# Half of x transposed by VectorE and by transfers inside SBUF, in a spectral mix with a dense layer

## The chip, the core and the metric

The kernel runs on one core of one Trainium2 chip. The metric is the device time of one execution in microseconds, the median of several runs. The engines are TensorE (PE, with its weight loads shown as PEld), VectorE (DVE), ScalarE (ACT), GpSimd (POOL) and SyncE (SP); DMA transfers are issued from queues of SP, ACT and POOL and carried by 16 DMA engines that they share. SBUF is the memory that the engines work in, with 128 partitions; PSUM, in eight banks, receives what PE computes.

## The reference

```
g = sigmoid((x * gate_w).sum(-1, keepdims=True))
a = irfft2(rfft2(x) * (w_r + 1j * w_i))          # over S = 2048 and D = 512
h = x @ w1 + b1                                  # D = 512 -> F = 1792
b = (h * tanh(softplus(h))) @ w2                 # Mish, F -> D = 512
out = g * a + (1 - g) * b
```

The kernel takes A_x for both branches. All inputs and the output are bfloat16.

## The kernel before

The 2048 rows of x lie in SBUF as 16 tiles of 128 rows (`xo`, 128 partitions x 16 x 512). Both branches need x transposed, with the 512 features on partitions: `xT` holds four blocks of 128 features (even and odd features of the two halves of D), each 2048 columns long. PE makes it (L466 to L482): for each pair of tiles, eight transposes of 128x128 (L476) into a PSUM bank, and an eviction on VectorE, or on ACT for some of the first (`evx`, L480).

**The dense branch** runs in four chunks of 512 rows (four tiles each). For a chunk, 14 groups of four matmuls (`mm1`, L773, contraction over the four feature blocks) give h in a bank; ACT adds the bias and applies Mish (L788) and writes `act`, which has three slots, so chunk c uses slot c % 3. Then for each tile, 14 matmuls (`mm2`, L803) with w2; the result is scaled by 1 - g (`bev`, L755) into `xo`.

**The spectral branch** splits the transform. Sums and differences of the two halves of `xT` (`ts`, `td`, L497) go to `Tb`, four tiles at a time. Then the row stage (`a1`, L512), whose two parts are added and subtracted on VectorE (`e1`, L525), the first column stage (`s1`, L538), an eviction to `Ybuf` (`e2`, L543) and writes to the scratch `scr1` in HBM (L547). When all are written, they are read back in another layout (L619) for the second column stage (`s2`, L635), the product with the filter on VectorE and POOL (L672 to L685), the inverse of it (`s2i`, L695), another trip through HBM (`scr2`, L705 and L710), and for each tile the last inverse stages (`s1i`, L723; `a1i`, L734), two scaled sums on VectorE (L745) and two additions on POOL (L751), which leave g * a in `ga`. A last addition (`sum`, L823) and a store (L760) end a tile; tiles 14 and 15 end with `fin` (L815).

**The gate** is one product with a running sum for each tile on VectorE (`gdot`, L553), a power on POOL (L559) and three small operations on VectorE; everything that scales by g or 1 - g waits for them.

**The order** is written down, not computed here. Every operation is a task with its engine, its dependences and the banks that it may use. The string `ORDER` (L258) lists all tasks in one sequence, two digits each, with the engine where there is a choice and the bank where one is taken; `schedule` (L216) reads it, and each engine runs its tasks in that sequence, waiting on semaphores for what a task needs. Each queue issues its transfers in the same way, so a transfer that has to wait holds up those behind it on its queue. SP issues nearly all loads, all scratch transfers and all stores; ACT's queue issues three of the w1 loads, POOL's one small load of the bias.

The loads on SP begin with tiles 0 to 1 and 2 to 3 of x, the constants `FMs`, a part of w1, tiles 4 to 7 and 8 to 11, two more parts of w1, and tiles 12 to 15. Then come the constants `GMs`, the gate's weights, 18 loads of the filter (`WT`, whole rows on every other one of 32 partitions), a part of `rt`, and w2 in two halves.

Of the kernel before, what the change touches and what calls it, by code (L numbers as in the profile page):

```python
# [13 lines left out]
NT = 16  # L14
# [151 lines left out]
class _Graph:  # L166
# [91 lines left out]
ORDER = (  # L258
    "0M0N0U047050P060O07080Q2z09000S0A010R0B0C0D0T020E0F030V0G0H0W0I0J0X0x60z50Y0yv0Z0K10v1146v212v1H30a1366l51I6q0"
    "14v0L7011Jv6m6n6w1Kv0b716o0c726p731L40d1M36r1N0e1W50f6s6t741Ov1V70g1560h1Pv1X6x0i6y6u16v7510j1Qa1Zv6z0k1701av1"  # L260
    "971Yv77318v761R41Av781B61Sv7920l0m0n7B01fv7A0o7D10p7C1gv0q1D70r1Cv7E1h30s1r42j1s61j7F20t21v0u1Ev7H00v22v1i17G1"
    "T7J31kv7I1U1lv2451F27K7L01mv1t1Gv2371uv7N47M1vv252Ov7O7b127v1wa2D37c2k28a26v7d07f22Nv7e2l1b67g1n42m2E11ca7h22F"
    "7j01d1ov1e7i1x62Hv7k1p342922Gv1ya1q7l52Av2Ia2Q41z2P17m2Z67n0202n2R2b2B2J22Tv7o2a72C2Sv7p12Ka2Uv2cv7r67q2dv2L2V"
    "27s2M2ev7t02Wv2f67u7v12o2X2ga2p7x52Y7w2h2q7z07y2i2r816802s8F1822t3578H48G362u398J28I373A8L58K2v3B8N63C388M0w8P"
    "18O2w8R28Q2x8T02y8S3D4308U3E63Mv8V38X13Nv8W8Y3Rv3Pg313F7P03G323Qv3Og7Q333H3Tg3Z33Sg7Ra3a13b8Z63iv3I57S08a3mv3J"
    "3jv7T3K3L3U3nv3kg3V47Ua7V33c3Xa3Wv3d3pg3Y3e03v43f3og3w644v7W3lg3x3y49v7Y13g7Xv3z3h3q45v7Z48v46g4028307aa4147g3"
    "r4843ta4Bg3sv4Ag3u4H485a4I24Qv86642434J4K4C4Uv4L874Rv89188a4Vv4Sg4D44Wg4M38b24Ea4N4Fa4Tg8c8A4G4Xg8d74O8Ba4P4Y8"
    "C08e4Z28f14av4ba8D8g4c8t18Ev8v28u8x08w4d8z18y4e9124f904g933929549497096992989B79A4h39C4p59D04qv4ia4x64r59E4yv4"
    "j75534s5D45L156a5Ev5T04z65Ma8h24u504t4k5Uv4wg5N14m5F34vg525V55O8i4l9fv5G5Q4ng515b78k04og8jv5W5P54g5I5Sg5H5768l"
    "5ca9ev5853g9g599F75Rg5A8mv5Kg9H49G5Y5Cg5d65X9J09I9hv5e9lv5j45r39K5Jg8n75sv5ka5Bg9kv5g5z35ag9m6745f5l568a5t19iv"  # L270
    "8o60v5m5hg9j5u5o5ig5v6908pa6F45n5Zg6135w8q26Ga5qg629nv6A645pg8r6B9ov635xg9p6C6N46V59qv6Oa9L78sv5yg6Wa66g6P69rv"
    "6X46Q6H26Eg6d09s6Y9M6S6I6Dg6R6ea6K65g6J9O19Nv6Ug6a6Mg6Z9P9uv9tv6cv9v6f56Tg9Qa9R46bv6g9xv6h6Lg9S6i9wv6kv9y9V06j"
    "g9T9U9Y29W9b79X9Z9a9c9d"
)
NBF = 14
GD_N = 8
E2P = 2.2
# [14 lines left out]
def _build(nc, A_x, A_w_r, A_w_i, B_x, B_w1, B_b1, B_w2, gate_w, out):  # L292
# [8 lines left out]
    with es:  # L301
        def sb(name, shape, dt):
            return es.enter_context(nc.sbuf_tensor(name, shape, dt))

        xo = sb("xo", [128, NT, 512], BF)
        xT = sb("xT", [128, 4, NT * 128], BF)
        Tg = sb("Tg", [128, 8192], BF)
# [40 lines left out]
        TT = Zb[:].rearrange("p a b c d e -> p (a b c d e)")[:, 0:2048].rearrange("p (s j n) -> p s j n", s=4, j=4)  # L348
        junk = Tg[:, 6144:6656]
# [38 lines left out]
        def mm(n):  # L388
            return n / 2400.0 + 0.0025
# [10 lines left out]
        def pe(name, dur, fn, **kw):  # L400
            return G.add(name, "pe", dur, fn, lat=0.17, **kw)
# [63 lines left out]

        for t0, h in ((0, 0), (0, 1), (2, 0), (2, 1), (4, None), (6, None), (8, None), (10, None), (12, None), (14, None)):  # L466
            pt = _Ps(SPEC[::-1])
            hs = (0, 1) if h is None else (h,)
            c0, nc_ = 2 * hs[0], 2 * len(hs)

            def f_tr(e, t0=t0, c0=c0, nc_=nc_, pt=pt):
                ins = None
                for i in range(2):
                    for c in range(c0, c0 + nc_):
                        o, d0 = ((c - c0) * 2 + i) * 128, 256 * (c // 2) + c % 2
                        ins = e.transpose(psb[:, pt.bank, o:o + 128], xo[:, t0 + i, d0:d0 + 255:2], ident[:, :])  # L476
# [14 lines left out]
        for t in range(NT):  # L491
            if t % 4 == 0:
                G.cur_prio = PR["sp"] + 0.9
                h = t // 4
                cols = slice(512 * h, 512 * h + 512)
                for (nm, o, op) in (("s", 0, ALU.add), ("d", 2, ALU.subtract)):
                    tt(f"t{nm}{h}", lambda o=o, hb=h % 2: Tb[:, hb, o:o + 2, :], lambda cols=cols: xT[:, 0:2, cols],  # L497
                       lambda cols=cols: xT[:, 2:4, cols], op, 1024, rate=2.0,
                       reads=[("xT", 4 * h + i, q) for i in range(4) for q in range(2)], writes=[("T", h % 2, nm)])
            if t % 2 == 0:  # L500
# [3 lines left out]
                for half in range(2):  # L504
                    pa = pas[half]

                    def f_a1(e, pa=pa, hb=hb, t=t, half=half):
                        ins = None
                        for i in range(2):
                            j0 = 128 * (t % 4 + i)  # L510
                            for r in range(2):
                                ins = e.matmul(ps[:, pa.bank, 256 * i:256 * i + 256].rearrange("p (s m) -> p s m", s=4)[:, r:4 - r:3 - 2 * r, :],  # L512
                                               Tb[:, hb, 2 * r + half, j0:j0 + 128], FMs[:, 2 * half + r, :], start=True, stop=True)
                        return ins

                    pe(f"a1{half}_{t}", 4 * mm(128), f_a1, reads=[("T", hb, "s"), ("T", hb, "d"), "FD"], writes=[("pa", t, half)], alloc=pa,
                       deps=e1s.get(t - 4, ()) if half == 0 else (), prio=PR["sp"] + 0.1 - 0.1 * half)
# [33 lines left out]
        for t in range(NT):  # L551
            G.cur_prio = PR["gate"] if t >= GD_N else 60.0
            G.add(f"gdot{t}", "dve", dve_dur(512),  # L553
                  lambda e, t=t: e.scalar_tensor_tensor(out=junk, in0=xo[:, t, :], scalar=1.0, in1=gwb,  # L554
                                                        op0=ALU.mult, op1=ALU.mult, accum_out=gdot[:, t:t + 1]),
                  reads=[("x", t), "gw"], writes=[("gd", t), "junk"], lock=True, deps=e1s[14] if t >= GD_N else ())

# [206 lines left out]
        for c in range(NCH):  # L764
            hb = c % 3
            G.cur_prio = PR["mm1"] - c
            for ft in range(NFT):
                pd = _Ps(DENSE[c])

                def f_mm1(e, c=c, ft=ft, pd=pd, cols=(0, 512), ks=range(4)):  # L770
                    ins = None
                    for i in ks:
                        ins = e.matmul(ps[:, pd.bank, cols[0]:cols[1]], w1_sb[:, i, 128 * ft:128 * (ft + 1)], xT[:, i, 512 * c + cols[0]:512 * c + cols[1]],  # L773
                                       start=(i == 0), stop=(i == 3))
                    return ins
# [8 lines left out]
                else:  # L784
                    pe(f"mm1_{c}_{ft}", 4 * mm(512), f_mm1, reads=[("xT", 4 * c + i, q) for i in range(4) for q in range(2)] + [("w1", ft, 0), ("w1", ft, 1)],
                       writes=[("pm", c, ft)], alloc=pd, deps=mm2s.get(c - 3, ()), prio=pr_m)
                G.add(f"mish_{c}_{ft}", "act", act_dur(512, True),
                      lambda e, ft=ft, pd=pd, hb=hb: e.activation(act[:, hb, ft, :], ps[:, pd.bank, :], AF.Mish, bias=b1f[:, ft:ft + 1]),  # L788
                      reads=[("pm", c, ft), "b1f"], writes=[("act", hb, ft)], frees=[pd], prio=PR["mish"])
            G.cur_prio = PR["mm2"] - c  # L790
            for tl in range(4):
                t = 4 * c + tl

                for part in range(len(LAST) if t == NT - 1 else 2):
# [5 lines left out]
                    def f_mm2(e, tl=tl, hb=hb, pd=pd, cs_=cs_, fts=fts):  # L800
# [8 lines left out]
                       writes=[("pd", t, part if t == NT - 1 else 0)],  # L809
                       alloc=pd if part == 0 or t == NT - 1 else None, deps=(mm2s[c][-1:] if t == NT - 1 and part else []))  # L810
                    mm2s.setdefault(c, []).append(tk)
# [126 lines left out]
```

## Time and profile before

| | us |
|---|---|
| median of 3 runs | 129.52 (129.48 to 129.56) |
| the profiled execution: span from its first to its last instruction | 128.0 |
| PE busy | 124.4 |
| VectorE busy | 92.2 |
| ACT busy | 68.9 |
| POOL busy | 54.4 |

The profile is one execution; its span leaves out what lies around the instructions, so it is shorter than the time of a run. A row of a group gives the line and the engine, what it writes and reads, the shape, how often, then the busy time in all and the mean of one in nanoseconds, and the idle time in front with what ended it. A piece of the chain of waits gives its start, its length and what it was, with the number of instructions merged into it. Spans of neighbouring instructions on an engine overlap: the mean of one is longer than the step from one start to the next. A row of a timeline has the start and the length first, and in brackets the idle time before. A row of a table by stages gives the stretch, its length, then the busy time of PE, PE's weight loads, VectorE, ACT and POOL with the number of instructions, the granted clock, the share of time in which the DMA engines are busy, and GB/s.

### The profile page before, as it was taken

The numbers are of one execution on the slowest core, as the hardware profiler recorded it, in microseconds if no ns is written. First come the engines' busy times: TensorE is split into PE (matmuls) and PEld (weight loads), VectorE is DVE, ScalarE is ACT, GpSimd is POOL, SyncE is SP. The second block draws the span as 40 slices with busy tenths as digits, with TensorE's granted clock in tenths as the row PEclk, the third lists the DMA queues.
The fourth block names the chain that finished last, engine by engine and source line by source line (L and its number), as shares of the span: only waits on it lengthen the run. The fifth ranks groups of instructions, "written<-read, shape, count | busy, mean of one in ns | idle before, by whom it ended". The sixth has DMA issues, their size and how long they took to land.

```text
span 128.0 us, 2725 instructions
## 1 busy us (share of the span) xinstructions
PE 124.4 (97%) x1046; PEld 67.9 (53%) x1046; DVE 92.2 (72%) x176; ACT 68.9 (54%) x113; POOL 54.4 (42%) x82
## 2 busy tenths in 40 slices
PE   7899999999999999999999999999999999999992
PEld 5698566545444444444444444444674457464482
DVE  0359997999989929998957900500399799999872
ACT  1339377889978784224024274487873475462300
POOL 4000000001000996979688394000038986998120
DMA  3999999999976398002304105449600204022231
GB/s 76 346 390 394 303 185 185 173 272 354 334 235 202 99 384 356 0 0 61 108 0 133 38 0 164 133 104 351 239 0 5 82 0 164 3 87 82 82 123 41
DMA packets 18653, 20.11 MB, mean 157 GB/s; under 512 B 1488, under 2 KB 15696, under 8 KB 18512
## 3 DMA queue, kind: packets, MB, share of 16 engines
q1 hardware_dynamic: 17792, 19.15, 49.7%
q10 hardware_dynamic: 816, 0.79, 1.9%
q8 instruction: 8, 0.13, 0.5%
q14 instruction: 5, 0.04, 0.1%
q0 software_dynamic: 32, 0.00, 0.0%
HBM read 13.64 MB, written 6.29 MB: 156 GB/s over the span
## 4 chain that ended last, share of the span: by engine, by line
PE 94%; DMA 3%; SPq 0%; DVE 0%; issue 0%
PE ps L803 38%; PE ps L773 38%; DMA xo<-in_A_x_dram 3%; PE ps L734 3%; PE ps L723 3%; PE ps L512 3%; PE ps L538 3%; PE ps L476 3%; PE ps L695 2%; PE ps L635 2%; SPq L374 0%; DVE xo L815 0%; PE ps L652 0%; PE ps L484 0%; PE ps L425 0%
## 5 line engine op out<-in xcount | busy, mean ns | idle before, releaser
L773 PE MATMUL ps<-xT,w_sb 128*128 128x512 bf16 (+1 forms) x240 | 52.9, 365 | 0.0
L803 PE MATMUL ps<-w_sb,act 128*128 128x512 bf16 (+2 forms) x252 | 51.6, 355 | 0.0
L788 ACT ACTIVATE act<-ps,b1f 128x512 bf16<-128x512 f32 x56 | 38.4, 688 | 18.5 <-PE ps L773 17.3
L803 PEld LDWEIGHTS ps<-w_sb,act 128*128 128x128 bf16 x252 | 22.7, 98 | 22.3 <-issue 0.8
L773 PEld LDWEIGHTS ps<-xT,w_sb 128*128 128x128 bf16 x240 | 22.3, 98 | 21.2 <-issue 0.6
L409 POOL TENSOR_TENSOR Tg<-Qb 128x256 bf16<-128x256 f32 x29 | 22.1, 790 | 21.9 <-DVE Qb L745 21.8
L409 POOL TENSOR_TENSOR Zb<-Qb 128x510 bf16<-128x510 f32 x16 | 19.8, 1268 | 5.1 <-DVE Qb L409 5.0
L409 DVE TENSOR_TENSOR Qb<-ps,WT 128x1024 f32<-128x1024 f32 x16 | 18.8, 1213 | 3.4 <-PE ps L635 3.4
L755 ACT ACTIVATE xo<-ps,omg 128x512 bf16<-128x512 f32 x8 | 5.5, 687 | 18.4 <-PE ps L803 10.1
L745 DVE SCALAR_TENSOR_TENSOR Qb<-ps,gcol,Qb 128x256 f32<-128x256 f32 x32 | 13.7, 475 | 1.5 <-ACT Qb L739 1.0
L404 DVE CAST Ybuf<-ps 128x1024 bf16<-128x1024 f32 x7 | 8.6, 1222 | 7.1 <-PE ps L695 6.7
L409 DVE TENSOR_TENSOR Abuf<-ps,Tg 128x512 bf16<-128x512 f32 x16 | 10.4, 685 | 2.4 <-PE ps L512 2.1
L576 POOL COPY wrv<-WT 128x32 bf16<-128x32 bf16 x2 | 0.4, 223 | 26.1 <-DMA WT<-in_A_w_i_dram 26.1
L405 ACT ACTIVATE Ybuf<-ps 128x1024 bf16<-128x1024 f32 x9 | 9.1, 1021 | 4.3 <-PE ps L695 4.3
L554 DVE SCALAR_TENSOR_TENSOR Tg<-xo,Tg 128x512 bf16<-128x512 bf16 x16 | 11.0, 688 | 0.3
L404 DVE CAST Zb<-ps 128x512 bf16<-128x512 f32 x6 | 4.1, 687 | 8.9 <-PE ps L723 8.9
L404 DVE COPY xT<-ps 128x1024 bf16<-128x1024 bf16 (+1 forms) x10 | 5.6, 579 | 5.4 <-PE ps L476 5.4
L409 DVE TENSOR_TENSOR xo<-xo,Tg 128x512 bf16<-128x512 bf16 x14 | 8.5, 615 | 0.3 <-ACT xo L755 0.3
L739 ACT ACTIVATE Qb<-ps,gcol 128x256 f32<-128x256 f32 x16 | 7.0, 475 | 2.7 <-PE ps L734 1.6
L405 ACT ACTIVATE Zb<-ps 128x512 bf16<-128x512 f32 x10 | 5.7, 596 | 4.6 <-PE ps L723 3.2
L598 POOL TENSOR_TENSOR ch<-wq 128x32 f32<-128x32 f32 x1 | 0.6, 624 | 12.5 <-DVE wq L593 12.5
L476 PE MATMUL ps<-ident,xo 128*128 128x128 bf16 x64 | 5.1, 225 | 0.5 <-DMA xo<-in_A_x_dram 0.5
(59 smaller groups left out, 92.8 us busy)
## 6 DMA issues: line engine op xcount, KB each, us to landing
Abuf<-scr SPq DMA_DIRECT2D x8, 512.0 KB, 5.4
scr<-Ybuf SPq DMA_DIRECT2D x16, 128.0 KB, 3.9
scr<-Ybuf SPq DMA_DIRECT2D x4, 512.0 KB, 3.8
w_sb<-in_B_w_dram SPq DMA_DIRECT2D x2, 896.0 KB, 13.6
out_dram<-xo SPq DMA_DIRECT2D x7, 256.0 KB, 2.0
xo<-in_A_x_dram SPq DMA_DIRECT2D x3, 512.0 KB, 7.7
rt<-c_rt SPq DMA_DIRECT2D x2, 512.0 KB, 8.5
WT<-in_A_w_r_dram SPq DMA_DIRECT2D x7, 128.5 KB, 10.4
```

The lines of the kernel that those rows point to most:

```text
L404: fs = {"dve": ("dve", dve_dur(n, rate=rate), lambda e: e.tensor_copy(out=dst(), in_=src())), "act": ("act", act_dur(n), lambda e: e.activ ...
L405: "act": ("act", act_dur(n), lambda e: e.activation(dst(), src(), AF.Copy))}
L409: f = lambda e: e.tensor_tensor(out=o(), in0=i0(), in1=i1(), op=op)
L476: ins = e.transpose(psb[:, pt.bank, o:o + 128], xo[:, t0 + i, d0:d0 + 255:2], ident[:, :])
L512: ins = e.matmul(ps[:, pa.bank, 256 * i:256 * i + 256].rearrange("p (s m) -> p s m", s=4)[:, r:4 - r:3 - 2 * r, :], Tb[:, hb, 2 * r + half ...
L554: lambda e, t=t: e.scalar_tensor_tensor(out=junk, in0=xo[:, t, :], scalar=1.0, in1=gwb, op0=ALU.mult, op1=ALU.mult, accum_out=gdot[:, t:t ...
L739: lambda e, t=t, sl=sl, p5=p5: e.activation(gC[:, sl, :].rearrange("p (i n) -> p i n", i=2), ps[:, p5.bank, :].rearrange("p (i n) -> p i n ...
L745: lambda e, t=t, sl=sl, p5=p5, o=o, op=op: e.scalar_tensor_tensor(out=st1[:, sl, o::2, :], in0=ps[:, p5.bank, :].rearrange("p (i n) -> p i ...
L755: G.add_multi(f"bev_{t}", [("act", act_dur(512, True), lambda e: e.activation(xo[:, t, :], ps[:, pd.bank, :], AF.Copy, scale=omg[:, t:t + ...
L773: ins = e.matmul(ps[:, pd.bank, cols[0]:cols[1]], w1_sb[:, i, 128 * ft:128 * (ft + 1)], xT[:, i, 512 * c + cols[0]:512 * c + cols[1]], sta ...
L788: lambda e, ft=ft, pd=pd, hb=hb: e.activation(act[:, hb, ft, :], ps[:, pd.bank, :], AF.Mish, bias=b1f[:, ft:ft + 1]),
L803: ins = e.matmul(ps[:, pd.bank, cs_], act[:, hb, ft, 128 * tl:128 * (tl + 1)], w2_sb[:, ft, cs_], start=(ft == 0), stop=(ft == NFT - 1))
```

## The change

Tiles 0 to 7 of x are still transposed by PE. Tiles 8 to 15 are transposed by VectorE in blocks of 32x32, one instruction for a tile, into a scratch that lies in slot 2 of `act` (the slot of chunk 2). Sixteen transfers of 64 KB inside SBUF then carry each group of 32 partitions of the scratch to the group of 32 partitions where it belongs in `xT`, eight issued on POOL's queue and eight on ACT's. Every one of them waits for all eight transposes.

`xT` is now two halves: `xTp` as before for tiles 0 to 7, and `xTb` for tiles 8 to 15, where the columns of a tile lie in four blocks of 32 by the group that they came from. What reads the second half follows: `mm1` of chunks 2 and 3 reads four runs of 128 columns and leaves its bank in that order, Mish reads the bank back in the order of rows, and the sums and differences `ts` and `td` of the second half are made in eight instructions of 512 columns (blocks of 32) instead of four of 1024. All of these wait for all sixteen transfers. The first eight Mish of chunk 2 wait for them too, since they write over the scratch.

Besides, the eight gate products that had to wait for the row stage need not any more, their scrap output has two buffers, and the pieces of tile 15's last `mm2` all come after the tile before. `ORDER` is new as a whole: the sequence on every engine, the banks, and the order of the loads. On SP the loads up to tiles 12 to 15 stay where they were; behind them the two halves of w2 and a part of `rt` come ahead of most of the filter loads, and the first writes to `scr1` stand between filter loads.

```
-        xT = sb("xT", [128, 4, NT * 128], BF)
+        xT = sb("xT", [128, 8192], BF)
...
+        xTp = xT[:, 0:4096].rearrange("p (q s) -> p q s", q=4)
+        xTb = xT[:, 4096:8192].rearrange("p (a q t j) -> p q a t j", a=4, q=4, t=8)
+        Zb32 = act[:, 2].rearrange("p f s -> p (f s)")[:, 0:4096]
+        Zw = Zb32.rearrange("p (b h e t j) -> p t h b e j", b=4, h=2, e=2, t=8)
...
-        for t0, h in ((0, 0), (0, 1), (2, 0), (2, 1), (4, None), (6, None), (8, None), (10, None), (12, None), (14, None)):
+        for t0, h in ((0, 0), (0, 1), (2, 0), (2, 1), (4, None), (6, None)):
...
+        for t in range(8, NT):
+            G.add(f"tp{t}", "dve", dve_dur(512), lambda e, t=t: e.transpose(
+                Zw[:, t - 8], xo[:, t, :].rearrange("p (b j e) -> p b e j", b=8, e=2)),
+                reads=[("x", t)], writes=[("Z", t)])
+        shs = []
+        for b in range(4):
+            for a in range(4):
+                shs.append(dma(f"sh{b}{a}", xT[32 * b:32 * b + 32, 4096 + 1024 * a:5120 + 1024 * a], Zb32[32 * a:32 * a + 32, 1024 * b:1024 * b + 1024],
+                               reads=[("Z", t) for t in range(8, NT)], writes=[("xB", b, a)], nbytes=65536, queue=SHQ[b], tail=1.9, bw=250e3))
+        XB = [("xB", b, a) for b in range(4) for a in range(4)]
...
+                    for e_ in range(2):
+                        xs = [xTb[:, e_ + 2 * i, :, 4 * h - 8:4 * h - 4, :] for i in range(2)]
+                        tt(f"t{nm}{h}{e_}", lambda o=o, e_=e_, hb=h % 2: Tb[:, hb, o + e_, :].rearrange("p (t a j) -> p a t j", t=4, a=4),
+                           lambda xs=xs: xs[0], lambda xs=xs: xs[1], op, 512, rate=2.0,
+                           reads=XB, writes=[("T", h % 2, nm, e_)])
...
-            G.cur_prio = PR["gate"] if t >= GD_N else 60.0
+            G.cur_prio = PR["gate"]
...
-                        ins = e.matmul(ps[:, pd.bank, cols[0]:cols[1]], w1_sb[:, i, 128 * ft:128 * (ft + 1)], xT[:, i, 512 * c + cols[0]:512 * c + cols[1]],
+                        o = ps[:, pd.bank, cols[0]:cols[1]]
+                        ins = e.matmul(o if c < 2 else o.rearrange("p (a t j) -> p a t j", a=4, t=4), w1_sb[:, i, 128 * ft:128 * (ft + 1)],
+                                       xTp[:, i, 512 * c + cols[0]:512 * c + cols[1]] if c < 2 else xTb[:, i, :, 4 * c - 8:4 * c - 4, :],
...
+                          act[:, hb, ft, :].rearrange("p (t a j) -> p t a j", t=4, a=4),
+                          ps[:, pd.bank, :].rearrange("p (t a j) -> p t a j" if c < 2 else "p (a t j) -> p t a j", t=4, a=4),
...
+                      deps=shs if c == 2 and ft < 8 else ())
```

with `SHQ = ("pool", "act", "pool", "act")`.

More of the change, by code (lines that the diff above doesn't have):

```diff
@@ L496, in _build @@
                 for (nm, o, op) in (("s", 0, ALU.add), ("d", 2, ALU.subtract)):
-                    tt(f"t{nm}{h}", lambda o=o, hb=h % 2: Tb[:, hb, o:o + 2, :], lambda cols=cols: xT[:, 0:2, cols],
-                       lambda cols=cols: xT[:, 2:4, cols], op, 1024, rate=2.0,
-                       reads=[("xT", 4 * h + i, q) for i in range(4) for q in range(2)], writes=[("T", h % 2, nm)])
+                    if h < 2:
+                        tt(f"t{nm}{h}", lambda o=o, h=h: Tb[:, h, o:o + 2, :], lambda cols=cols: xTp[:, 0:2, cols], lambda cols=cols: xTp[:, 2:4, cols], op, 1024, rate=2.0,
+                           reads=[("xT", 4 * h + i, q) for i in range(4) for q in range(2)], writes=[("T", h, nm, e) for e in range(2)])
+                        continue
+                    for e_ in range(2):
[3 more added lines that the diff above has]
+                           reads=XB, writes=[("T", h % 2, nm, e_)])
             if t % 2 == 0:
@@ L514, in f_a1 @@
                         return ins
-                    pe(f"a1{half}_{t}", 4 * mm(128), f_a1, reads=[("T", hb, "s"), ("T", hb, "d"), "FD"], writes=[("pa", t, half)], alloc=pa,
+                    pe(f"a1{half}_{t}", 4 * mm(128), f_a1, reads=[("T", hb, nm, half) for nm in "sd"] + ["FD"], writes=[("pa", t, half)], alloc=pa,
                        deps=e1s.get(t - 4, ()) if half == 0 else (), prio=PR["sp"] + 0.1 - 0.1 * half)
@@ L784, in _build @@
                 else:
[L785 removed]
+                    pe(f"mm1_{c}_{ft}", 4 * mm(512), f_mm1, reads=(XB if c >= 2 else [("xT", 4 * c + i, q) for i in range(4) for q in range(2)]) + [("w1", ft, 0), ("w1", ft, 1)],
                        writes=[("pm", c, ft)], alloc=pd, deps=mm2s.get(c - 3, ()), prio=pr_m)
                 G.add(f"mish_{c}_{ft}", "act", act_dur(512, True),
[L788 to L789 removed]
+                      lambda e, c=c, ft=ft, pd=pd, hb=hb: e.activation(
+                          act[:, hb, ft, :].rearrange("p (t a j) -> p t a j", t=4, a=4),
+                          ps[:, pd.bank, :].rearrange("p (t a j) -> p t a j" if c < 2 else "p (a t j) -> p t a j", t=4, a=4),
+                          AF.Mish, bias=b1f[:, ft:ft + 1]),
+                      reads=[("pm", c, ft), "b1f"], writes=[("act", hb, ft)], frees=[pd], prio=PR["mish"],
+                      deps=shs if c == 2 and ft < 8 else ())
             G.cur_prio = PR["mm2"] - c
@@ L809, in _build @@
                        writes=[("pd", t, part if t == NT - 1 else 0)],
[L810 removed]
+                       alloc=pd if part == 0 or t == NT - 1 else None, deps=(mm2s[c][-1:] if t == NT - 1 else []))
                     mm2s.setdefault(c, []).append(tk)
```

40 lines of the change are left out of this document (20 added, 20 removed).

## The prediction

> **What bounds the kernel now.** I read the page's totals first, then the granted clock, then the chain of waits.
>
> ```profile
> span 128.0 us, 2725 instructions
> PE 124.4 (97%) x1046; PEld 67.9 (53%) x1046; DVE 92.2 (72%) x176; ACT 68.9 (54%) x113; POOL 54.4 (42%) x82
> PE 94%; DMA 3%; SPq 0%; DVE 0%; issue 0%
> core 0: 128.0 us, clock 1.000
> ```
>
> A busy PE alone proves little, as matmul spans overlap. But the chain that ended last runs through PE for 94% of the span, at a full clock, so its start-to-start times are the price of each matmul:
>
> ```profile
> 5.57 0.40 PE ps L476 x4
> 7.12 1.75 PE ps L773 x16
> 10.42 0.45 PE ps L476 x8
> 36.51 0.43 PE ps L538 x2
> 36.94 4.32 PE ps L773 x20
> 47.36 0.56 PE ps L635 x32
> 90.83 0.45 PE ps L723 x8
> 119.56 6.13 PE ps L803 x56
> ```
>
> A 512-column matmul costs 4.32/20 = 0.216 us, a 256-column one 1.75/16 = 0.109, a transpose or other 128-column one 0.45/8 = 0.056. From 5.57 us the chain never leaves PE until 125.69 (119.56 + 6.13). So a matmul less is time less, as long as nothing makes PE wait. The only large hole is at the start, where PE waits for tiles 2 and 3 of x:
>
> ```profile
> 4.88 0.22 PE L425 MATMUL ps<-const-bfloat16-1.0 128*128 128x128 bf16 x1
> 5.57 0.40 PE L476 MATMUL ps<-ident,xo 128*128 128x128 bf16 x4 [0.48 <-DMA xo<-in_A_x_dram]
> ```
>
> **The change, part by part.** First, what leaves PE: eight tiles of four transposes, 32 x 0.056 = 1.79 us. Four of VectorE's ten evictions go with them. Second, the new order puts four 256-column matmuls (0.44 us) ahead of the transposes of tiles 2 and 3, inside that hole. They need the first half of w1, which came through ACT's queue:
>
> ```profile
> L374 ACTq DMA_DIRECT2D w_sb<-in_B_w_dram x3: 621/627/633, 0.8 to 2.1; - x3
> DMA to landing us min/median/max: 4.2/4.9/6.5
> ```
>
> The first was issued at 0.80 and landed at 0.80 + 4.2 = 5.0, so they run from 5.0 to 5.5 and the hole shrinks by about 0.44. PE's sum falls by 1.79 + 0.44 = 2.23.
>
> Third, what is added off PE. These are the rows nearest to each piece of work:
>
> ```profile
> L554 DVE SCALAR_TENSOR_TENSOR Tg<-xo,Tg 128x512 bf16<-128x512 bf16 x16 | 11.0, 688 | 0.3
> L404 DVE COPY xT<-ps 128x1024 bf16<-128x1024 bf16 x6 | 4.0, 683 | 0.0
> L409 DVE TENSOR_TENSOR Tg<-xT 128x1024 bf16<-128x1024 bf16 x8 | 5.3, 683 | 0.0
> L404 DVE COPY xT<-ps 128x512 bf16<-128x512 bf16 x4 | 1.6, 422 | 5.4 <-PE ps L476 5.4
> L404 DVE CAST Ybuf<-ps 128x1024 bf16<-128x1024 f32 x7 | 8.6, 1222 | 7.1 <-PE ps L695 6.7
> ```
>
> The trace has no transpose on VectorE. [...] I take 0.69, the gate's product, which like it handles 512 bf16 columns with no doubled rate. The eight cost 5.5 us; the evictions give back 4 x 0.683 = 2.7. The sums and differences of the second half become eight of 512 columns instead of four of 1024: 8 x 0.42 - 4 x 0.683 = +0.6 if their blocks of 32 columns keep the pace, +2.7 at 0.683 each. VectorE gains 3.4 us in all.
>
> Whether that costs time is a question of the feed. The sixteen transfers can start only when tile 15 is transposed. The loads ahead of the last x load on SP's queue are the same and in the same order, so I keep its landing:
>
> ```profile
> 5.47 0.78 SPq L374 DMA_DIRECT2D xo<-in_A_x_dram  x1
> DMA to landing us min/median/max: 9.5/9.5/9.5
> ```
>
> It lands at 5.47 + 9.5 = 15.0. VectorE's order puts the first four transposes before that and four behind it: 15.0 + 4 x 0.69 = 17.7. [...] Eight transfers then go out on POOL's queue, eight on ACT's with five Mish (128x512) among them:
>
> ```profile
> L374 POOL DMA_DIRECT2D braw<-in_B_b_dram x1: 785/785/785, 1.3 to 1.3; - x1
> braw<-in_B_b_dram POOLq DMA_DIRECT2D x1, 3.5 KB, 4.4
> L788 ACT ACTIVATE act<-ps,b1f 128x512 bf16<-128x512 f32 x56 | 38.4, 688 | 18.5 <-PE ps L773 17.3 <-PE ps L654 0.6 <-PE ps L585 0.2
> out_dram<-xo SPq DMA_DIRECT2D x1, 64.0 KB, 1.5
> ```
>
> POOL, at the one issue that the trace has: last issue at 17.7 + 7 x 0.785 = 23.2, landed 4.4 later, 27.6. That load had 14 rows, a transfer has 32, so the issue may cost up to 0.785 x 32/14 = 1.79; then 34.6. I take 0.8 to 1.0, nearer the row (29.1 at 1.0). ACT: last issue at 17.7 + 7 x 0.627 + 5 x 0.688 = 25.5. A landing takes between 1.5 (64 KB on idle engines) and 4.9 (256 KB on ACT's queue beside SP's loads); I take 2.5, since 64 KB is a quarter of that: 28.0, bounds 27.0 and 30.4.
>
> And the demand: in the new order PE has 78 matmuls of 512 columns, 28 of 256 and 52 of 128 between 5.57 and the first that reads tiles 8 to 15 (Matmult of chunk 2): 16.85 + 3.05 + 2.91 = 22.8 us, so it wants them at 28.4. Supply 28.0, demand 28.4: hidden, with half a microsecond to spare. If it is late, PE stalls at that matmul, its queue behind it holds the stage-one matmuls, and every microsecond passes to the end, because nothing later is slack. VectorE waits at the same point, with the stage-one evictions queued behind it. ACT's first issue waits on the transposes, with Mish of chunks 0 and 1 and so PE's banks behind it; it stands behind enough Mish to come up at about 17.7.
>
> [...]
>
> Fourth, what is moved. The column stage now ends later (laid out by the prices above, its last matmul ends at about 47, against 36.94), and PE has 44 matmuls of 512, 9.5 us, until it wants the data read back from scr, where before it had 10.4 (36.94 to 47.36). The chain there is an eviction of 1.0 to 1.2, two writes on SP and a read:
>
> ```profile
> L374 SPq DMA_DIRECT2D scr<-Ybuf x4: 615/616/617, 38.0 to 40.0; - x4
> DMA to landing us min/median/max: 2.1/2.2/2.6
> DMA to landing us min/median/max: 4.0/4.0/4.0
> ```
>
> (the last is the first read, Abuf<-scr at 42.3). 1.2 + 0.6 + 0.6 + 2.2 + 4.0 = 8.6: covered. The w2 loads move ahead of most filter loads on SP; the late filter loads have until about 49.7, when in the same layout the small filter matmul comes up. In the last stage PE's work from the first inverse matmul to the end falls from 34.9 (90.83 to 125.69) to about 28.3, while VectorE and POOL keep theirs:
>
> ```profile
> L409 POOL TENSOR_TENSOR Tg<-Qb 128x256 bf16<-128x256 f32 x29 | 22.1, 790 | 21.9 <-DVE Qb L745 21.8
> L745 DVE SCALAR_TENSOR_TENSOR Qb<-ps,gcol,Qb 128x256 f32<-128x256 f32 x32 | 13.7, 475 | 1.5 <-ACT Qb L739 1.0 <-PE ps L734 0.3 <-issue 0.2
> L409 DVE TENSOR_TENSOR xo<-xo,Tg 128x512 bf16<-128x512 bf16 x14 | 8.5, 615 | 0.3 <-ACT xo L755 0.3
> ```
>
> VectorE there: 13.7 + 8.5, five evictions (3.4), two adds (1.2), one scaling (0.75), the four last pieces (1.9): 29.5 busy, about 27 with the overlap of neighbours. It is as full as PE. So I take 0.6 of the 2.23 back for the tail and small waits (bounds 0 and 1.6). The profiled span was 128.0 and the median of the runs 129.52, 1.5 around it. Sum: 129.5 - 2.23 + 0.6 = **127.9**.
>
> **The rivals.** *Late feed* (the other side): POOL's software issue is the one price with wide bounds. At 1.79 us the last transfer lands at 34.6, PE stalls 6.2, and the time is 127.9 + 6.2 = 134; at 1.3 it lands at 31.2, stalls 2.8, 130.7. From 1.2 us an issue on (2 us of stall), the change loses. For it: 32 rows, DMA engines that are full in just this stretch, and at only 193 GB/s while narrow loads run (16 to 28 us):
>
> ```profile
> 1.00:16.00 15.00, 14.52 (x132) 10.84 (x131) 9.03 (x17) 6.74 (x12) 1.41 (x5) 1.00 0.97 322
> 16.00:28.00 12.00, 12.00 (x93) 6.93 (x92) 11.22 (x23) 9.45 (x17) 0.00 (x0) 1.00 1.10 193
> ```
>
> [...]
>
> *Slow sums*: blocks of 32 columns lose the double rate; 2.1 us more on VectorE between the transfers and the column stage, about half of it behind PE's other work: 127.9 + 1.0 = 128.9. Against it, nothing in the trace; for it, no row has such blocks.
>
> *The gain is eaten at the end*: VectorE, not PE, ends last. If its 27 us of the last stage start no earlier against PE and lose another 1.0 to 1.6 to POOL, the result is 128.9 to 129.6, say 129.3. For it: the sums on VectorE take 615 ns on average though one alone is shorter, while POOL runs beside them.
>
> **How the numbers follow.** Forecast 0.42, slow sums 0.10, late feed 0.33, tail 0.15. Some 0.2% (0.26 us) is what a measurement here can tell from no change. Faster: 0.42 + 0.10 + 0.05 of the tail + 0.02 of a slight late feed = 0.59. Same: 0.05 + 0.02 = 0.07. Slower: 0.29 + 0.05 = 0.34. The range runs from 127.2 (all of the 2.23 kept) to 133.0, which leaves out the upper end of the late feed; the forecast's own range is 127.2 to 128.9.
>
> **What would show it.** Right: L476's successor has 32 matmuls on PE; eight VectorE transposes of about 0.69 us, the last ending near 17.7; POOL issues of 0.8 to 1.0; the first chunk-2 matmul starting near 28.4 without a wait on a DMA; the last matmul ending near 123.5. Wrong: a PE wait on xT's transfers, POOL issues over 1.2, transposes over 1 us, or a last VectorE piece that ends more than 1 us behind the last matmul. A gain with a stall at 28 would mean that I priced PE's part too low.

## The result, and the profile after

| | before | after |
|---|---|---|
| median of the runs | 129.54 us | 135.88 us (135.42 to 137.25) |
| ratio | | 1.0501, 95% interval 1.0447 to 1.0554 |
| profiled span | 128.0 us | 133.7 us |

The change makes the kernel 5% slower; 127.9 was predicted. The ratios here leave disturbed, longer executions out and the medians don't, so the two can differ, and the profiled executions of E5, E7, E8 and E9 are of that longer kind.

The page of the changed kernel: totals, granted clock, and the shares of the chain that ended last.

```profile
span 133.7 us, 2728 instructions
PE 124.4 (93%) x1014; PEld 66.9 (50%) x1014; DVE 89.5 (67%) x174; ACT 71.1 (53%) x122; POOL 57.5 (43%) x91
PE 81%; DVE 7%; DMA 6%; ACTq 1%; issue 1%; ACT 1%; DVEq 1%
core 0: 133.7 us, clock 0.980
```

PE carried 94% of the chain before; now DMA and VectorE have a part in it, and the clock is no longer full. Three pieces of that chain (start, length, what) and PE's timeline show where (in this kernel `mm1` is L795, `a1` L533, `mm2` L830, the transfers L379, VectorE's transposes L489, `fin` L842, the scaled sums L766, `sum` L414):

```profile
24.47 8.19 DMA xT<-act
33.14 3.41 PE ps L795 x8
36.78 1.73 PE ps L795 x8
```

```profile
28.67 0.39 PE L533 MATMUL ps<-FMs,Tg 128*128 128x128 bf16 x4
33.14 3.41 PE L795 MATMUL ps<-xT,w_sb 128*128 128x512 bf16 x8 [4.08 <-DMA xT<-act]
```

The last transfer was issued at 24.47 and landed 8.19 us later. PE came to the first matmul of chunk 2 at 29.06 and waited 4.08. And the eight matmuls that follow take 3.41, though the next eight take 1.73: 1.68 more. The table by stages gives the reason in its granted clock, the third number from the end:

```profile
28.50:33.20 4.70, 0.62 (x7) 0.35 (x6) 0.23 (x1) 1.70 (x3) 0.00 (x0) 0.96 1.19 253
33.20:36.60 3.40, 3.40 (x12) 1.28 (x13) 2.80 (x8) 1.48 (x3) 0.00 (x0) 0.55 0.92 219
36.60:50.00 13.40, 13.40 (x90) 7.08 (x88) 11.01 (x21) 9.95 (x19) 0.74 (x2) 1.00 0.31 85
```

Behind the 4.08 us of idle time the clock stands at 0.55 for 3.4 us, and from 36.6 to 50 us at 1.00.

The transposes and transfers, in the view of one line (durations in ns: least, median, most; then the first and last start in us):

```profile
L489 DVE STREAM_TRANSPOSE act<-xo x8: 669/669/711, 10.9 to 16.3; 128x512 bf16<-128x512 bf16 x8
L379 POOL DMA_DIRECT2D xT<-act x8: 496/496/577, 17.2 to 20.8; - x8
L379 ACTq DMA_DIRECT2D xT<-act x8: 514/610/739, 17.4 to 24.5; - x8
DMA to landing us min/median/max: 5.9/7.3/8.3
```

All eight transposes are done at 17.0, and POOL issues a transfer in half a microsecond. It is the landing that is long. The DMA view of the stretch from 17.3 to 21.7 us (queues with what they moved, then what was issued) tells what they wait for:

```profile
q1 hardware_dynamic: 1334, 1.30, 110.7%
xT<-act POOLq DMA_DIRECT2D x8, 64.0 KB, 6.2
xT<-act ACTq DMA_DIRECT2D x3, 64.0 KB, 6.5
```

Eleven of the sixteen transfers had been issued, yet SP's queue (q1) is the only one that moved anything: 1.30 MB, w2 and filter loads that SP had issued before. From 21.8 on the queues of POOL (q0) and ACT (q10) move too. Not all that SP had issued went first, though. The sizes of its loads add up to some 6.15 MB issued by 17.3, and its queue had moved 5.59 by 21.7; the second half of w2 landed at 29.0, the first of the transfers at 23.2. The rest of SP's loads moved beside the transfers.

The last stage, from the first inverse matmul to PE's last: before, after; then VectorE's last piece before, and the last pieces of VectorE and PE after.

```profile
90.83:125.69 34.86, 34.84 (x285) 21.04 (x281) 30.41 (x62) 16.27 (x33) 22.08 (x29) 1.00 0.18 68
```

```profile
101.42:129.36 27.94, 27.94 (x253) 17.84 (x249) 26.27 (x54) 17.68 (x36) 23.58 (x30) 1.00 0.20 74
```

```profile
125.71 0.35 DVE L815 SCALAR_TENSOR_TENSOR xo<-ps,omg,Tg 128x128 bf16<-128x128 f32 x1 [0.43 <-PE ps L803]
```

```profile
128.40 1.28 DVE L414 TENSOR_TENSOR xo<-xo,Tg 128x512 bf16<-128x512 bf16 x2
129.60 1.65 DVE L842 SCALAR_TENSOR_TENSOR xo<-ps,omg,Tg 128x512 bf16<-128x512 f32 x4
```

```profile
120.06 9.30 PE L830 MATMUL ps<-w_sb,act 128*128 128x512 bf16 x70
```

PE ends at 129.36, VectorE at 131.25, 1.89 behind; before, VectorE's last piece ended at 126.06 (125.71 + 0.35), 0.37 behind PE's last matmul. So the difference of the spans, 5.7, is: -2.23 saved on PE (the forecast's sum; E4 below measures 2.24), +4.08 of waiting, +1.68 of half clock, +1.52 between PE's end and VectorE's, and +0.51 from VectorE's last piece to the end of the span (2.45 against 1.94), where the last stores stand. The other 0.14 lies in gaps on PE too small for a view to list them.

### The profile page after: what moved, and what is told of

Same layout as the page of the kernel before. It is cut to its first block, busy times and chain, and to the rows that moved or that the text cites. A ratio compares the mean times of both kernels' runs of the same rounds, so it can differ in the third digit from the quotient of the medians.

```text
span 133.7 us, 2728 instructions
## 1 busy us (share of the span) xinstructions
PE 124.4 (93%) x1014; PEld 66.9 (50%) x1014; DVE 89.5 (67%) x174; ACT 71.1 (53%) x122; POOL 57.5 (43%) x91
## 4 chain that ended last, share of the span: by engine, by line
PE 81%; DVE 7%; DMA 6%; ACTq 1%; issue 1%; ACT 1%; DVEq 1%
PE ps L795 33%; PE ps L830 30%; DMA xT<-act 6%; PE ps L430 3%; PE ps L755 3%; PE ps L744 3%; DVE xo L414 3%; DVE Qb L766 2%; PE ps L559 2%; PE ps L533 2%; PE ps L716 2%; PE ps L481 2%; PE ps L656 2%; ACTq L379 1%; DVE Tg L414 1%
## 5 line engine op out<-in xcount | busy, mean ns | idle before, releaser
L795 PE MATMUL ps<-xT,w_sb 128*128 128x512 bf16 (+1 forms) x240 | 54.6, 373 | 4.1 <-DMA xT<-act 4.1
L830 PE MATMUL ps<-w_sb,act 128*128 128x512 bf16 (+2 forms) x252 | 51.7, 356 | 0.0
L811 ACT ACTIVATE act<-ps,b1f 128x512 bf16<-128x512 f32 x56 | 35.8, 689 | 25.3 <-PE ps L795 24.0
L795 PEld LDWEIGHTS ps<-xT,w_sb 128*128 128x128 bf16 x240 | 22.8, 100 | 26.4 <-issue 6.3
L830 PEld LDWEIGHTS ps<-w_sb,act 128*128 128x128 bf16 x252 | 22.9, 98 | 23.4 <-issue 0.8
L414 POOL TENSOR_TENSOR Tg<-Qb 128x256 bf16<-128x256 f32 x30 | 23.6, 819 | 16.4 <-DVE Qb L766 16.3
L414 POOL TENSOR_TENSOR Zb<-Qb 128x510 bf16<-128x510 f32 x16 | 20.0, 1268 | 0.0
L414 DVE TENSOR_TENSOR Qb<-ps,WT 128x1024 f32<-128x1024 f32 x16 | 18.7, 1212 | 0.0
L776 ACT ACTIVATE xo<-ps,omg 128x512 bf16<-128x512 f32 x13 | 8.8, 690 | 13.1 <-PE ps L830 10.7
L766 DVE SCALAR_TENSOR_TENSOR Qb<-ps,gcol,Qb 128x256 f32<-128x256 f32 x32 | 13.7, 473 | 1.4 <-ACT Qb L760 1.4
L414 DVE TENSOR_TENSOR Abuf<-ps,Tg 128x512 bf16<-128x512 f32 x16 | 10.5, 686 | 3.1 <-PE ps L533 2.1
L379 POOL DMA_DIRECT2D xT<-act x8 | 4.0, 507 | 14.5 <-DVE act L489 14.5
L409 DVE CAST Zb<-ps 128x512 bf16<-128x512 f32 x5 | 3.3, 681 | 10.1 <-PE ps L744 10.1
L414 DVE TENSOR_TENSOR Tg<-xT 128x512 bf16<-128x512 bf16 (+1 forms) x12 | 5.6, 507 | 5.9 <-DMA xT<-act 5.4
L414 DVE TENSOR_TENSOR xo<-xo,Tg 128x512 bf16<-128x512 bf16 x14 | 9.0, 664 | 0.0
L489 DVE STREAM_TRANSPOSE act<-xo 128x512 bf16<-128x512 bf16 x8 | 5.1, 680 | 2.3 <-DMA xo<-in_A_x_dram 2.3
## 6 DMA issues: line engine op xcount, KB each, us to landing
scr<-Ybuf SPq DMA_DIRECT2D x16, 128.0 KB, 2.2
WT<-in_A_w_r_dram SPq DMA_DIRECT2D x7, 128.5 KB, 10.0
```

The costliest lines, as they stand in the source:

```text
L379: t = G.add(name, queue, issue if issue != 0.62 or queue != "pool" else 1.0, lambda e: e.dma_start(dst, src), reads=reads, writes=writes, ...
L409: fs = {"dve": ("dve", dve_dur(n, rate=rate), lambda e: e.tensor_copy(out=dst(), in_=src())), "act": ("act", act_dur(n), lambda e: e.activ ...
L414: f = lambda e: e.tensor_tensor(out=o(), in0=i0(), in1=i1(), op=op)
L489: G.add(f"tp{t}", "dve", dve_dur(512), lambda e, t=t: e.transpose(Zw[:, t - 8], xo[:, t, :].rearrange("p (b j e) -> p b e j", b=8, e=2)), ...
L766: lambda e, t=t, sl=sl, p5=p5, o=o, op=op: e.scalar_tensor_tensor(out=st1[:, sl, o::2, :], in0=ps[:, p5.bank, :].rearrange("p (i n) -> p i ...
L776: G.add_multi(f"bev_{t}", [("act", act_dur(512, True), lambda e: e.activation(xo[:, t, :], ps[:, pd.bank, :], AF.Copy, scale=omg[:, t:t + ...
```

## The experiments

Theory A: the transfers wait behind what SP has already queued, on whatever queue they are issued. Theory B: the transfers, or the queues of POOL and ACT, are slow in themselves. All four first runs are the changed kernel with one edit.

**E1.** SP's first w2 load, and so all behind it, waits for the sixteen transfers.

```
         order = G.schedule()
+        by = {t.name: t for t in G.tasks}
+        by['ld_w2_0'].deps += shs
```

> The changed kernel with one wait added: SP issues the first half of w2 (and so all that stands behind it on its queue) only when all sixteen transfers have landed. Theory A (backlog: the transfers wait behind the loads that SP had already queued, w2 and rt above all): each transfer lands within 3 us of its issue instead of 6 to 8, the last by 27 us instead of 32.7, PE does not wait at the first matmul of chunk 2, the clock stays 1.0, and the span falls by the 4.1 us of the wait and the 1.7 us of the slow clock to about 128, the time to about 129.7. Theory B (the transfers themselves are slow, narrow and inside SBUF, or the two queues are): landings stay at 6 to 8 us, the wait stays above 3 us, time 135 or more.

Measured: 130.36 us, ratio 1.0046 (1.0018 to 1.0074). Transfers in the view of their tile:

```profile
DMA to landing us min/median/max: 1.9/2.0/2.6
```

Same transfers, same queues, 2.0 instead of 7.3, and PE doesn't wait on them: theory B falls. The time is 0.7 above the 129.7 that theory A gave. What is left above the kernel before stands at the end: PE's last matmul ends at 124.77, VectorE at 126.65.

**E2.** w2 and a part of `rt` behind SP's first write.

```
+        for n in ['ld_w2_0', 'ld_w2_1', 'ld_ri']:
+            order['sp'].remove(by[n])
+        i0 = order['sp'].index(by['ld_Wm01'])
+        order['sp'][i0:i0] = [by[n] for n in ['ld_w2_0', 'ld_w2_1', 'ld_ri']]
```

> The changed kernel with the two halves of w2 and the second part of rt moved on SP's queue behind the first write to scr1 (issued at about 24 us). No wait is added; seven filter loads stay ahead. Theory A: the backlog that the transfers meet ends at about 20.7 us instead of 22 and is not followed by w2; the last lands at 27 to 29, PE waits less than 1 us, span about 128.5, time about 130. Theory B: no gain, 135 or more.

Measured: 131.33 us, ratio 1.0104 (1.0075 to 1.0133).

```profile
DMA to landing us min/median/max: 1.9/2.2/5.7
```

The last transfer, issued when w2 had begun, is the slow one and lands at 30.0. VectorE waits 2.9 for it, and PE waits 1.6 at the first matmul of chunk 2, which starts at 30.48. So theory A's numbers (the last landing by 29, a wait on PE under 1 us, 130 us) were missed.

**E3.** Twenty matmuls of constants (512 columns) fill PE's wait; their bank is overwritten by the matmul that follows.

```
+                late = {d.sem.num for d in shs} if t.name == "mm1_2_1" else ()
+                for key, (sem_, val) in sorted(need.items(), key=lambda kv: kv[0] in late):
+                    if key in late and late:
+                        for _ in range(NDUM):
+                            eobj.matmul(ps[:, t.alloc[0].bank, :], nc.const_aps.tensor(1.0, [128, 128], BF), nc.const_aps.tensor(1.0, [128, 512], BF), start=True, stop=True)
+                        late = ()
```

> The changed kernel; behind the last stage-one matmul and ahead of the wait for the transfers PE runs 20 matmuls of 512 columns on constants into the bank that the first matmul of chunk 2 then overwrites (4.3 us of work that nothing uses). If the half clock from 33.2 to 36.6 us comes from PE's idle time before it, the clock stays at 1.0, the eight matmuls there take 1.7 us instead of 3.4, and the time falls by about 1.5 us to 134.3. If the clock falls for another reason, 135.9 to 136.5.

Measured: 134.96 us, ratio 1.0386 (1.0346 to 1.0425), 0.9 under the changed kernel. The same stretches of the table by stages:

```profile
28.50:33.20 4.70, 4.70 (x27) 2.21 (x25) 0.25 (x1) 1.85 (x4) 0.00 (x0) 1.00 1.15 258
33.20:36.60 3.40, 3.35 (x19) 1.69 (x19) 3.40 (x10) 2.04 (x4) 0.00 (x0) 1.00 0.90 215
```

With no idle stretch the clock stays at 1.00, and 3.4 us hold 19 matmuls instead of 12: the half clock comes from the wait. The landings stay as they were (5.8 to 8.5). Of the 1.68 us the whole kernel gets back less than was expected (0.9, not 1.5): behind these matmuls PE is 1.25 ahead (its next group starts at 35.14 instead of 36.39), but later it waits 0.6 for the first read back from scr, which lands only 0.3 earlier, and in the profiled executions its last matmul ends 0.5 earlier (128.84 against 129.36).

**E4.** ACT's eight transfers go out on SP, ahead of w2.

```
-SHQ = ("pool", "act", "pool", "act")
+SHQ = ("pool", "sp", "pool", "sp")
...
+        for n in ['sh10', 'sh33', 'sh32', 'sh13', 'sh12', 'sh11', 'sh30', 'sh31']:
+            order['sp'].remove(by[n])
+        i0 = order['sp'].index(by['ld_w2_0'])
+        order['sp'][i0:i0] = [by[n] for n in ['sh10', 'sh33', 'sh32', 'sh13', 'sh12', 'sh11', 'sh30', 'sh31']]
```

> The changed kernel with the eight transfers of ACT issued on SP's queue instead, ahead of w2, so that SP waits for the transposes (17.2 us) before it goes on, and ACT is free of eight issues (5 us of issue time between its Mish). Theory A: what SP had queued drains by about 20 us, the transfers land by 23 to 24, no wait at chunk 2, w2 starts at about 21; span about 127.5, time about 129. Theory B: the last lands after 30, time 134 or more.

Measured: 129.73 us, ratio 0.9996 (0.9971 to 1.0021), span 127.8. The transfers (issued, landed), then the last rows of PE and VectorE:

```profile
L379 SPq DMA_DIRECT2D xT<-act x8: 577/592/599, 17.3 to 21.7; - x8
DMA to landing us min/median/max: 2.0/2.5/2.8
```

```profile
114.15 9.30 PE L830 MATMUL ps<-w_sb,act 128*128 128x512 bf16 x69
123.68 1.64 DVE L842 SCALAR_TENSOR_TENSOR xo<-ps,omg,Tg 128x512 bf16<-128x512 f32 x4
```

All have landed at 24.1 and PE waits for none. POOL's eight still go out on POOL's queue (median landing 2.3), so that queue isn't what made them late. PE's last matmul ends at 123.45, 2.24 earlier than before the change: PE's part of the gain is there. But VectorE ends at 125.32, 1.87 behind it instead of 0.37, which gives 1.50 back, and the span ends 2.48 behind VectorE instead of 1.94, which gives back another 0.54. So theory A's 129 was missed.

**E5.** In what unit do transfers wait? The changed kernel with each half of w2 in seven loads.

```
...
+                for k in range(7 * h, 7 * h + 6):
+                    e.dma_start(w2_sb[:, k, :], w2v[:, k, :]).then_inc(sem, 16)
+                return e.dma_start(w2_sb[:, 7 * h + 6, :], w2v[:, 7 * h + 6, :])
...
```

> The changed kernel, but each half of w2 (896 KB) goes out as seven transfers of 128 KB instead of one; order, queues and all else as in the changed kernel. It asks in what unit the 16 transfers of xT wait behind the loads on SP. Theory A1, that a queue keeps the DMA engines until the transfer that it is in has ended and then gives a turn to the other queues: the 16 transfers start to move within about 1 us of their issue (about 18.5, not 22), land about 2 to 4 us after it, the last at about 28, and the wait at the first matmul of chunk 2 falls from about 4 us to under 1; time 130 to 131.5. Theory A2, that whatever SP had issued earlier is carried first, however it is cut: seven issues take SP about 4.3 us in place of one, so a few of the later loads fall behind the transfers, but those issued before 17.3 (all of w2's first half and some of its second) still go first, the transfers start at about 21 to 22, and the time stays within 1 us of the changed kernel's 135.9. Both keep the tail, so neither goes under 129.5.

Measured: 136.54 us, ratio 1.0453 (1.0416 to 1.049). The DMA view from 18.1 to 21.9 us shows one queue again:

```profile
q1 hardware_dynamic: 1326, 1.18, 111.5%
w_sb<-in_B_w_dram SPq DMA_DIRECT2D x4, 128.0 KB, 7.8
xT<-act POOLq DMA_DIRECT2D x8, 64.0 KB, 6.7
xT<-act ACTq DMA_DIRECT2D x3, 64.0 KB, 7.0
```

This is A2's side: loads of 128 KB hold the transfers up as loads of 896 KB do (median landing 7.1 us, against 7.3), and no other size was tried. What counted here is how much was queued ahead, though not to the last byte, as the second half of w2 showed above. In the trace before, two queues with loads from about the same moment on did move side by side: from 5 to 6 us ACT's queue moved 0.21 MB and SP's 0.15. Here the transfers didn't move for 4 us. Which part of the machinery keeps the order isn't shown.

**E6.** On E4: in the last stage, five evictions and one scaling from VectorE to ACT.

`e5` are the evictions of the inverse stage (those that ACT already had stay there), `bev_7` is the scaling.

```
-                t.eng, t.dur, t.fn = next(o[:3] for o in t.opts if o[0] == ENGINE[ORDER[pos]])
+                t.eng, t.dur, t.fn = next(o[:3] for o in t.opts if o[0] == OVR.get(t.name, ENGINE[ORDER[pos]]))
...
+OVR = {'e5_0': 'act', 'e5_1': 'act', ... 'e5_15': 'act', 'bev_7': 'act'}
```

> The version with ScalarE's eight transfers issued on SP ahead of w2 (129.7 us, span 127.8), and in the last stage the VectorE evictions of the inverse stage's PSUM banks (L409, five, 0.68 us each) and one scaling (L777, 0.74 us) go to ScalarE; all in the same sequence. Theory T1, that VectorE's sum of work from about 96 us on sets the end (it runs back to back and ends 1.9 us behind the last matmul): 4.1 us of work leave it, its end moves to that of PE's last pieces, span 126.0 to 126.6, time 127.9 to 128.5. Theory T2, that POOL's additions (30 of 0.82 us, the last ending at 123.1) or their sharing with VectorE set the end: VectorE waits for them instead, and span and time stay within 0.4 us of 127.8 and 129.7. If ScalarE, which then has the evictions behind its Mish and its scaled copies, holds up PE, PE's last matmul ends later than 123.5.

Measured: 130.95 us, ratio 1.01 (1.0082 to 1.0119). VectorE's first scaled sums and its last rows, E4 and then E6:

```profile
97.89 0.88 DVE L766 SCALAR_TENSOR_TENSOR Qb<-ps,gcol,Qb 128x256 f32<-128x256 f32 x2 [0.18 <-ACT Qb L760]
```

```profile
99.70 1.71 DVE L767 SCALAR_TENSOR_TENSOR Qb<-ps,gcol,Qb 128x256 f32<-128x256 f32 x4 [13.74 <-ACT Qb L761]
...
125.17 1.65 DVE L843 SCALAR_TENSOR_TENSOR xo<-ps,omg,Tg 128x512 bf16<-128x512 f32 x4
```

```profile
115.54 9.30 PE L831 MATMUL ps<-w_sb,act 128*128 128x512 bf16 x69
```

4.1 us of work left VectorE, and it ended 1.5 later (126.82 against 125.32): ACT, loaded more, brought its first sums 1.8 later, and PE's last matmul came 1.4 later. T1, the sum of VectorE's work, falls as I put it (127.9 to 128.5 was expected), and so does T2's time (within 0.4 of 129.7); what came is the case that the expectation named last, ACT holding up PE. It suggests that what counts is when VectorE's work can begin and whether it then runs without gaps.

**E7 to E12.** E4 with other ORDER strings, the same work on the same engines. They were laid out from E4's own durations and landings. The edit of E11:

```
 ORDER = (
-    "0M0N0420P0O0Q05060R0U070T08090A020V0B0C0D0E0S0F0G000H010I0x40yv0J030K0z00L7F17A313511610a1X77K4752767B12a7C7G7"
+    "04205060708090A0B0C0D0E0F0G0H0I0N0O0S0U0200010M0P0Q0R0T0V0W0X0Y0Z0a0b0l0f0r0c0x40J0K0z00L0310a0yv7F17A31351161"
...
```

> The version with eight of the transfers on SP ahead of w2 (129.7 us, span 127.8), the same operations, engines, banks and queues, with a new ORDER laid out from durations and landings of that version's own trace. Theory T3, that what ends it is the length of the spectral chain after the late xT (VectorE's 27 us of the last stage can start only when the second read from HBM has landed, 94.9), so that spectral work put ahead of the gate's products and of dense matmuls on PE, and fewer long waits in the last stage, take back the 1.9 us by which VectorE ends behind PE: the first inverse matmul at 94.0 to 95.0, PE's last matmul at 123.3 to 123.8, VectorE's last piece within 0.8 us of it, span 126.2 to 126.8, time 127.9 to 128.6. Theory T4, that VectorE and POOL, sharing what they share, are full in the last stage whatever the order: VectorE still ends 1.5 us or more behind PE, time 129.3 to 130.

> As the run before it, with another ORDER of the same kind, in which the last x tile's transpose comes 2 us later and the second read from HBM about 0.5 us earlier. T3: time 127.8 to 129, and whichever of the two has the earlier inverse stage ends earlier. T4: 129.3 to 130, as the other.

Measured: 143.99 us, ratio 1.102 (1.0964 to 1.1076), and 136.04, ratio 1.0296 (1.0233 to 1.036). Both moved ACT's w1 loads back, and PE waited for them at the start (E7: 8.48 and 4.78 us; E8: 5.2): nothing on T3 or T4.

> As the two runs before it, which PE began with waits of 8.5 and 4.8 us (the second, of 5.2 us) for w1: their ORDER had moved ScalarE's three w1 loads behind other work, so they told nothing on the last stage. Here everything that starts before 15.5 us keeps its place. T3 (a matter of order): no wait for loads at the start, the first inverse matmul at 93.5 to 95.5, PE's last matmul at 123.2 to 124, VectorE's last piece within 0.8 us of it, span 126.2 to 127, time 127.9 to 128.8. T4 (VectorE and POOL full in the last stage whatever the order): VectorE ends 1.5 us or more behind PE, 129.3 to 130.

> As the run before it with another ORDER of the kind; here w2's second half is issued at about 30 and lands last of the loads, so PE may wait for it near 38, which would show as a wait on w2. Without that wait T3 gives 127.9 to 128.8, T4 129.3 to 130.

Measured: E9 134.25 us, ratio 1.007 (1.0042 to 1.0097), E10 133.44, ratio 1.0267 (1.0234 to 1.0299). Each has one wait on PE, for a half of w2, and the row by stages around it, E9 first:

```profile
41.47 2.86 PE L830 MATMUL ps<-w_sb,act 128*128 128x512 bf16 x7 [4.06 <-DMA w_sb<-in_B_w_dram]
```

```profile
36.00:50.00 14.00, 9.94 (x51) 4.54 (x50) 7.14 (x12) 4.86 (x10) 0.41 (x2) 0.88 0.69 173
```

```profile
40.41 1.68 PE L830 MATMUL ps<-w_sb,act 128*128 128x512 bf16 x7 [3.17 <-DMA w_sb<-in_B_w_dram]
```

```profile
36.00:50.00 14.00, 10.83 (x63) 5.33 (x62) 10.02 (x20) 7.03 (x14) 0.41 (x2) 1.00 0.69 180
```

Behind the wait of 4.06 the clock is low again (seven matmuls in 2.86, and 0.88 over the 14 us of the row), behind the one of 3.17 it isn't (1.68 and 1.00). T3's times were missed in both; for E10 the wait for w2's second half had been named as a risk. In these profiles VectorE ends 1.05 (E9) and 0.39 (E10) behind PE.

> A fifth ORDER of the version with eight transfers on SP ahead of w2 (129.7 us, span 127.8). All loads and transfers keep the sequence of that version, as the two runs before lost 4.1 and 3.2 us to a wait for w2, which their ORDER had put behind most of the filter's loads; beside those waits PE had no gap left, and VectorE ended 1.05 us (not 1.9) behind PE in the first. T3 (the tail is a matter of order): no DMA wait on PE, the first inverse matmul at 94 to 95.5, PE's last matmul at 122.8 to 123.8, VectorE's last piece 0.6 to 1.1 us behind, span 126 to 127, time 127.7 to 128.7. T4 (VectorE and POOL full whatever the order): VectorE ends 1.5 us or more behind PE, 129.3 to 130.

> As the run before it with another ORDER of the kind, the first inverse matmul about 0.9 us later: T3 127.9 to 129, about half a microsecond above the other; T4 129.3 to 130.

Measured: E11 128.83 us, ratio 0.994 (0.9917 to 0.9962), span 127.2; E12 129.56, ratio 0.999 (0.9968 to 1.0011). E11's last rows of PE and VectorE:

```profile
116.56 7.79 PE L830 MATMUL ps<-w_sb,act 128*128 128x512 bf16 x63
```

```profile
121.04 1.81 DVE L414 TENSOR_TENSOR xo<-xo,Tg 128x512 bf16<-128x512 bf16 x2
122.78 0.41 DVE L414 TENSOR_TENSOR Tg<-Qb 128x256 bf16<-128x256 f32 x1
123.11 1.65 DVE L842 SCALAR_TENSOR_TENSOR xo<-ps,omg,Tg 128x512 bf16<-128x512 f32 x4
```

The time is just above T3's 127.7 to 128.7. VectorE ends 0.4 behind PE, so the 1.87 wasn't fixed, which is T3's side. But most of that is PE: it ends at 124.35, 0.9 later than in E4 and later than T3 allowed, while VectorE ends 0.56 earlier (124.76 against 125.32). In E12 VectorE ends 0.75 behind PE, and yet the time stays in T4's range. E11 is the one version that beats both kernels, the first by 0.6%. T4 holds in part. VectorE's idle time in front of its scaled sums fell from 1.4 us in E4 to 0.5 in E11, but the fourteen sums, the same in both, became slower: eight of them are held up by one of POOL's additions in E4, twelve in E11 (the last section shows how this is seen; mean of one, E4 and then E11):

```profile
L414 DVE TENSOR_TENSOR xo<-xo,Tg 128x512 bf16<-128x512 bf16 x14 | 9.0, 664 | 0.0
```

```profile
L414 DVE TENSOR_TENSOR xo<-xo,Tg 128x512 bf16<-128x512 bf16 x14 | 11.0, 816 | 0.0
```

## Why the prediction was wrong

The forecast was 127.9 us; the measured 135.88 lies beyond the upper end of the range, 133.0. The step that failed is the landing of the transfers; two smaller terms, the price of lateness and the tail, were too low besides.

- *What leaves PE, 2.23 us.* Right. With the feed in time (E4) PE's last matmul ended at 123.45; 123.5 was forecast.
- *VectorE's transposes, 0.69 each, the last ending at 17.7.* Right: 0.67, 17.0, so the feed wasn't late by it.
- *The sums in blocks of 32 columns, 0.42.* Right; the rival of slow sums falls.

```profile
L414 DVE TENSOR_TENSOR Tg<-xT x12: 414/420/692, 7.2 to 39.3; 128x512 bf16<-128x512 bf16 x8, 128x1024 bf16<-128x1024 bf16 x4
```

- *POOL's issue, 0.8 to 1.0.* Wrong, but on the kind side: 0.50. The late feed was priced through it, from 1.2 us an issue on; the feed was late with an issue of half a microsecond.
- *The landing, 1.5 to 4.9 with 2.5 taken (4.4 on POOL).* This is the step that failed. I took rows in which little was queued ahead and sized by bytes, though my own row of 16 to 28 us had the DMA engines full (1.10). Even so my figure for POOL's transfers at 1.0 us an issue was 29.1, past the demand of 28.4; the supply of 28.0 was ACT's alone. By then SP had both halves of w2 and filter loads in its queue, which the new order had moved there; I listed that move as one of the late filter loads and didn't ask what it does to transfers on other queues. Measured 5.9 to 8.3; E1 and E4 show 2.0 and 2.5 with nothing large queued ahead. So the supply was 32.7 instead of 28.0, against a demand of 29.06 (28.4 forecast).
- *The price of lateness, one for one.* Too low by 1.68 on PE: after 4.08 us of waiting the clock stood at 0.55 for 3.4 us, and without the idle stretch at 1.00 (E3, which got 0.9 of it back).
- *The tail, 0.6.* Too low. In E4 VectorE's end stands 1.5 further behind PE than before, and the span's end another 0.54 behind that: 2.04 of the 2.24. The reason was in the prediction, in the rival of the gain that is eaten at the end: VectorE's 27 us against PE's 28.3. I gave it a chance of 0.15 and took it for a size that might be off. E6 and E11 point to a chain: in E4 the first part of the second read from HBM lands at 94.9 and VectorE's first scaled sum starts at 97.89, where before the change these were 88.2 and 93.90, and from there to the end it has 1.4 us of idle time in E4. How much of the rest is order and how much is VectorE and POOL holding each other up isn't settled: no run separates the two.
- *The column stage and the trip through scr* were covered as forecast; PE's longest wait for the data read back was 0.4 us in E1, 0.6 in E3 and 0.8 in E5.

The rival of the late feed had the place right. At a landing of 32.7 its own pricing would have given 127.9 + 4.3 = 132.2; half clock (1.68) and the part of the tail beyond 0.6 (1.43 of 2.03) make up 3.1 of the other 3.7 to 135.9. The range ended at 133.0 because it left out that rival's upper end, and in the rival's price a wait cost no more than itself. The place was right partly by luck: that rival had it through POOL's issue, and the cause was the backlog.

## What to carry to other kernels

A small transfer on its own queue isn't ahead of the large loads that another queue has already issued, as far as these runs show (landings of 5.9 to 8.3 us behind such loads, 1.9 to 2.8 in E1 and E4): its landing has to be read from a row with the same backlog, and the cure is to issue it first (E4) or to hold the loads (E1), not to cut them (E5). A wait of 4.08 us on PE cost 1.68 us more here, at a clock of 0.55. Time taken from the engine that bounds is kept only if the chain through the others, here from the late data to VectorE's last stage, gets as much shorter; otherwise the order has to be laid out anew with measured landings, and even then the best of six orders kept only 0.8 of 2.2 us here.

## What the hardware showed that was not expected

- Transfers inside SBUF on two queues stood still for 4 us while a third queue drained (1.30 MB; E5: 1.18 MB), with that queue's w2 loads at 896 KB as at 128 KB.
- POOL's issue of 32 rows took 0.50, less than the 0.785 of the one load of 14 rows before.
- A wait of 3.17 us left the clock at 1.00 (E10, 36 to 50 us). Behind one of 4.08 it stood at 0.55 for 3.4 us, and behind one of 4.06 (E9) seven matmuls took 2.86 instead of 1.68. In E5's profile a wait of 4.19 cost more: the eight matmuls behind it took 3.57, with a clock of 0.50 from 33 to 37 us, and the next eight still 2.51 instead of 1.89.
- One sum of 512 columns on VectorE takes 0.41 undisturbed and up to 0.95 (E4 and E11) where it meets an addition of POOL's that is under way. E4, around 105 us, two sums and then the addition that the second one meets:

```profile
104.70 0.41 DVE L414 TENSOR_TENSOR xo<-xo,Tg 128x512 bf16<-128x512 bf16 x1
105.82 0.86 DVE L414 TENSOR_TENSOR xo<-xo,Tg 128x512 bf16<-128x512 bf16 x1
105.67 0.72 POOL L414 TENSOR_TENSOR Tg<-Qb 128x256 bf16<-128x256 f32 x1
```

The second sum ends 0.28 us behind the addition's end (0.29 by the rounded rows), and the same distance is found for eight of the fourteen sums in E4 and twelve in E11, though 0.27 to 0.66 of the addition was left when they started. What holds the sum back isn't shown.
